# A delta-rule attention feeding a softplus MLP on one core: the work up to the first MLP layer, put in another order

## The chip, the cores and the metric

The kernel runs on one core of one Trainium2 chip. The time is the device time of one execution in microseconds (us), lower is better. The engines are PE (TensorE, matmuls), DVE (VectorE), ACT (ScalarE), POOL (GpSimd) and SP (SyncE, which issues nearly all DMAs here). Each has its own instruction queue, taken strictly in order; semaphores tie them together.

## What is computed

```python
def _attn_ref(q, k, v, beta):              # q, k, v: (4, 8, 768, 48)
    k_n = k / (np.linalg.norm(k, axis=-1, keepdims=True) + 1e-06)
    state = zeros((B, H, D, D))
    for t in range(S):
        y[:, :, t] = einsum('bhd,bhde->bhe', q[:, :, t], state)
        v_old = einsum('bhde,bhd->bhe', state, k_n[:, :, t])
        state = state + beta[:, :, t] * outer(k_n[:, :, t], v[:, :, t] - v_old)
    return y

def _moe_ref(x, w_in, w_out):              # x: y as (3072, 384); w_in (384, 2048)
    h = x @ w_in
    g = np.maximum(h, 0.0) + np.log1p(np.exp(-np.abs(h)))
    return g @ w_out
```

## The kernel before

**Staging.** The 768 steps are cut into 12 chunks (`NS`) of 64 steps, for all 32 pairs of batch and head at once. Inside a chunk the recurrence is a triangular system of 64 by 64 per head. Two chunks share one `invert(u)`, which turns the 32 by 32 diagonal blocks of their systems into inverses on DVE, row by row; the off-diagonal blocks are added with matmuls. A chunk's result y goes as the input x into the MLP, which is `layer` s of the loops below: 16 pieces of the hidden dimension, two at a time, so eight groups g. For every group, `hidden(s, g)` multiplies x with two pieces of w_in, ACT and DVE make the softplus (`gh`), and `output(s, g)`, one group later, multiplies it with two pieces of w_out. The work of chunks s+1 and s+2 is planned into the groups of layer s by the table that `at(...)` fills.

**Before the first layer** nothing can be overlapped with an MLP: the code between `with tc.manual_schedule` and `plan = {}` does chunk 0 in the order in which it is written, which is the order on every engine. Its steps, with the tiles by which they are found in the trace: `gram_heads` (products of keys, tile `work`), `p_half` (queries by keys into `ph`), `invert(0)` (tiles `ltq`, `Z`, `tmp`), `finish(0)` (two transposes of `Z` into `tt`), `join(0)` (two sets of 128 matmuls that put the 16-wide halves of the inverse together; the first set is emptied by ACT into `w1`, tile `x`; a subtraction and a third transpose follow on DVE), `mask_p` (four products with `maskP` into `big`), `cross_a`, `arrange`, `cross_b` (off-diagonal blocks: matmuls into one PSUM tile `pa`, emptied in four pieces by ACT and DVE in turn; `arrange` copies on ACT and clears on POOL), `scale_v`, `u_all` (emptied into `big`), `y_all` (y into `x` and `x4`, then six DMAs that put x4's rows into x) and `state`.

**Three streams are threaded through this.** The weights of piece f come by two DMAs (`a`, `b`, 384 KB each); `top(f)` on ACT (two CASTs into `ex`) and `convert(f)` on DVE (two SCALAR_TENSOR_TENSOR into `a`) make floats of them. Two `ex` tiles serve all pieces in turn, so `top(f)` waits until `convert(f-2)` has read. `invert(1)` is a generator in `background`; `pull(budget)` takes steps from it, by costs in ns that are written at each `yield`, until the budget is used. In the first layers `room`, from `EARLY[s]`, is that budget for each group. A load of weights into a tile is set free by a one-column copy on DVE (`[:, 0:1]`, here a token).

**Names in the profile.** L180 transpose of `work`, L217 and L222 the two operations of an elimination step, L228 and L230 the transposes of `finish`, L249 and L250 the end of `join`, L241 and L248 its matmuls, L258 and L281 the matmuls of `cross_a` and `cross_b`, L264 and L266 and L285 their emptying, L272 `arrange`, L321 `mask_p`, L328 and L332 `u_all`, L355, L360 and L361 `y_all`, L371 its DMAs, L340 and L343 `state`, L397 `top`, L407 `convert`, L384 the token, L446 `hidden`, L450 to L452 and L463 the softplus of layer 0, L474 `output`.

Of the kernel before, what the change touches and what calls it, by code (L numbers as in the profile page):

```python
# [7 lines left out]
F32 = mybir.dt.float32  # L8
F32R = mybir.dt.float32r
I32 = mybir.dt.int32  # L10
# [3 lines left out]
AF = mybir.ActivationFunctionType  # L14
ALU = mybir.AluOpType
# [16 lines left out]
AHEAD = 5  # L32
N16 = 1
STEP, EARLY, PULL0 = 3100, (4100, 3500, 3500), (500, 500, 3000)
# [7 lines left out]
def deltanet_moe(ctx, tc, kT, qT, kI, vN, beta, wts, out):  # L42
# [65 lines left out]
    def parity(t):  # L108
        return t.rearrange("p (a e) c -> p e a c", e=2)
# [114 lines left out]

    def finish(u):

        tt = TT[u] = one.tile([P, 2 * NP, 2 * HB], F32, name="tt")
        nc.vector.transpose(tt[:, :, 0:HB].rearrange("p q c -> p c q"), Z)  # L228
        yield 2000
        nc.vector.transpose(tt[:, :, HB:].rearrange("p q c -> p c q"),  # L230
                            Z.rearrange("p c j -> p j c"))
        yield 2000
# [19 lines left out]

    def cross_a(s):

        tt = TT[s // 2][:, s % 2 * NP:(s % 2 + 1) * NP, :]
        pm = ps_a.tile([P, NP // 2, HB], F32, name="pa")
        for i, e, p, ab, t in quads:
            nc.tensor.matmul(pm[(lo, hi)[e][t], i, :], OFF[s][hi[t], p, :], tt[hi[t], p, 0:HB],  # L258
                             start=True, stop=True)
        for e in range(2):  # L260
            for t in range(2):
                o = parity(OFF[s])[lo[t], e]
                if s < 1 and t:
                    nc.vector.tensor_scalar(o, pm[(lo, hi)[e][t]], -1.0, None, op0=ALU.mult)  # L264
                else:
                    nc.scalar.activation(o, pm[(lo, hi)[e][t]], AF.Copy, scale=-1.0)  # L266

    def arrange(s):

        tt = TT[s // 2][:, s % 2 * NP:(s % 2 + 1) * NP, :]  # L270
        for h in range(2):
            nc.scalar.copy(tt[hi[h], :, HB:], tt[hi[h], :, 0:HB])  # L272
        for h in range(2):
            nc.gpsimd.memset(tt[hi[h], :, 0:HB], 0.0)

    def cross_b(s):

        tt = TT[s // 2][:, s % 2 * NP:(s % 2 + 1) * NP, :]
        pm = ps_a.tile([P, NP // 2, HB], F32, name="pa")
        for i, e, p, ab, t in quads:  # L280
            nc.tensor.matmul(pm[(lo, hi)[e][t], i, :], tt[lo[t], p, HB:], OFF[s][lo[t], p, :],  # L281
                             start=True, stop=True)
        for e in range(2):
            for t in range(2):
                copies[s < 1 and t](parity(tt)[lo[t], e, :, HB:], pm[(lo, hi)[e][t]])  # L285
# [32 lines left out]
    def mask_p(g, pt):  # L318
        gs = slice(8 * g, 8 * g + 8)
        for ab in range(2):  # L320
            nc.vector.tensor_tensor(  # L321
                bv[tk[ab], ab, gs, 0:C], pt[tk[ab]],
                maskP[tk[ab]].unsqueeze(1).to_broadcast([C, 8, C]), op=ALU.mult)
# [21 lines left out]
    def y_all(s):  # L345
# [34 lines left out]
    def load_weights(f):  # L380
        RA[f] = one.tile([P, 2 * DM], I32, name=f"a{f + 1}")
        RB[f] = one.tile([P, 2 * DM], I32, name=f"b{f}")
        if f >= AHEAD:
            nc.vector.tensor_copy(RA[f][:, 0:1], RA[f - AHEAD][:, 0:1])  # L384
        for i, t in enumerate((RA[f], RB[f])):
            nc.sync.dma_start(t.bitcast(U16)[:, 0:4 * DM - 1],
                              wts[f][:, 4 * DM * i + 1:4 * DM * (i + 1)])
# [11 lines left out]
    def convert(n=1):  # L399
        for _ in range(n):  # L400
            f = done[0]
            if f == NF:
                return
# [7 lines left out]
            if f + AHEAD < NF:  # L411
                load_weights(f + AHEAD)

    def top(n=1):
        for _ in range(n):
            if done[1] < NF:
                assert done[1] < done[0] + 2
                top_half(done[1])
                done[1] += 1
# [70 lines left out]
    done = [0, 0]  # L490
    background = []
# [16 lines left out]
    with tc.manual_schedule(engines={ET.PE, ET.DVE, ET.Activation, ET.Pool, ET.SP}):  # L508
# [4 lines left out]
        load_weights(0)  # L513
# [8 lines left out]
        load_weights(1)  # L522
# [33 lines left out]
        load_v(1)  # L556
        for f in range(2, AHEAD):
            load_weights(f)
        load_k(4)
        run(iv)  # L560
# [12 lines left out]
        pull(1)  # L573
        top()
        run(jn)
        pull(1)
        convert()
        cross_a(0)
        arrange(0)
        top()  # L580
        scale_v(0)
        pull(PULL0[0])
        cross_b(0)
        convert()
        top()
        pull(PULL0[1])
        u_all(0)
        load_v(2)
        pull(PULL0[2])
        y_all(0)  # L590
        convert()
# [6 lines left out]
        top()  # L598

# [89 lines left out]
        for s in range(NS):  # L689
            for g in range(NF // 2):  # L690
                cost, *blocks = plan.pop((s, g), (0, (), ()))
                highs, lows = [x.get(8 * s + g, ()) for x in (HIGHS, LOWS)]
                if s == 0:
                    convert(max(0, 2 * g + 2 - done[0]))
                hidden(s, g)
# [9 lines left out]
                if s == 0:  # L705
                    convert(2)
                    top(2)
# [63 lines left out]
```

## Time and profile before

| | |
|---|---|
| time, median of 3 runs | 593.34 us (589.03 to 593.53) |
| the profiled execution | 592.98 us |
| its span in the trace | 591.3 us |
| PE busy | 559.9 us (95%) |
| DVE busy | 447.9 us (76%) |
| ACT busy | 356.0 us (60%) |
| weights `a` and `b`, from issue to landing | 4.9 and 5.6 us |

The first matmul of layer 0 starts 54 us into the span. Times below are us from the start of the span; a busy time is that of the engine's instructions without its waits. The granted clock is a share of 2.4 GHz, so 0.50 is 1.2 GHz.

### The profile page before, as it was taken

The numbers are of one execution on the slowest core, as the hardware profiler recorded it, in microseconds if no ns is written. First come the engines' busy times: TensorE is split into PE (matmuls) and PEld (weight loads), VectorE is DVE, ScalarE is ACT, GpSimd is POOL, SyncE is SP. The second block draws the span as 40 slices with busy tenths as digits, with TensorE's granted clock in tenths as the row PEclk, the third lists the DMA queues.
The fourth block names the chain that finished last, engine by engine and source line by source line (L and its number), as shares of the span: only waits on it lengthen the run. The fifth ranks groups of instructions, "written<-read, shape, count | busy, mean of one in ns | idle before, by whom it ended". The sixth has DMA issues, their size and how long they took to land.

```text
span 591.3 us, 19891 instructions
## 1 busy us (share of the span) xinstructions
PE 559.9 (95%) x8630; PEld 523.3 (88%) x8630; DVE 447.9 (76%) x1003; ACT 356.0 (60%) x719; POOL 30.2 (5%) x55
## 2 busy tenths in 40 slices
PE   5757799999999999999999999999999999999996
PEld 5446577789999999999999999999999999999996
DVE  5988789678899998798888898797895554554442
ACT  4444768898547584556595556685545576444543
POOL 4210000000000000000010000000000000000000
PEclk9657799999999999999999999999999999999999
DMA  9924852301320202320301320300311200300000
GB/s 215 334 71 116 267 190 57 68 30 55 68 60 29 65 30 55 68 82 13 60 30 55 68 83 12 60 30 29 68 55 28 42 29 2 76 21 15 28 0 28
DMA packets 35320, 39.82 MB, mean 67 GB/s; under 512 B 22688, under 2 KB 25856, under 8 KB 35232
## 3 DMA queue, kind: packets, MB, share of 16 engines
q1 hardware_dynamic: 35232, 38.54, 24.8%
q8 instruction: 68, 1.11, 0.8%
q14 instruction: 20, 0.16, 0.1%
HBM read 31.55 MB, written 4.72 MB: 61 GB/s over the span
## 4 chain that ended last, share of the span: by engine, by line
PE 80%; DVE 10%; ACT 5%; issue 2%; DMA 1%; SPq 1%; ACTq 0%; DVEq 0%
PE po L474 33%; PE ph L446 32%; PE pa L355 3%; PE pa L294 3%; PE pa L328 2%; PE pa L340 2%; PE pa L124 2%; DVE ltq L180 1%; PE pa L258 1%; PE pa L281 1%; DVE a L457 1%; DMA kt<-kT 1%; DVE Z L222 1%; DVE tmp L217 1%; DVE ltq L194 1%
## 5 line engine op out<-in xcount | busy, mean ns | idle before, releaser
L446 PE MATMUL ph<-x,b 128*128 128x256 f32 x1056 | 193.3, 282 | 0.0
L446 PE MATMUL ph<-x,a 128*128 128x256 f32 x624 | 172.9, 300 | 1.8 <-DMA x<-x 1.6
L446 PEld LDWEIGHTS ph<-x,b 128*128 128x128 f32 x1056 | 168.1, 190 | 0.5
L450 ACT ACTIVATE a<-ph 128x512 f32<-128x512 f32 x96 | 57.5, 599 | 175.9 <-PE ph L446 175.7
L474 PE MATMUL po<-a,gh 128*128 128x384 f32 x416 | 143.4, 367 | 0.0
L474 PE MATMUL po<-b,gh 128*128 128x384 f32 x352 | 124.4, 354 | 3.2 <-DVE gh L459 2.9
L446 PEld LDWEIGHTS ph<-x,a 128*128 128x128 f32 x624 | 119.7, 192 | 6.9 <-DMA x<-x 1.8
L457 DVE SCALAR_TENSOR_TENSOR a<-ph,a 128x512 f32<-128x512 f32 x88 | 60.5, 687 | 59.0 <-ACT a L452 58.4
L474 PEld LDWEIGHTS po<-a,gh 128*128 128x128 f32 x416 | 78.9, 191 | 8.0 <-issue 1.8
L474 PE MATMUL po<-b,gl 128*128 128x384 f32 x352 | 77.0, 334 | 0.0
L474 PEld LDWEIGHTS po<-b,gh 128*128 128x128 f32 x352 | 66.1, 188 | 9.0 <-DVE gh L459 3.6
L460 DVE TENSOR_TENSOR gl<-a,gh 128x512 fp32r<-128x512 f32 x88 | 61.0, 693 | 3.0
L451 ACT ACTIVATE a<-a 128x512 f32<-128x512 f32 x96 | 60.7, 632 | 3.1
L452 ACT ACTIVATE a<-a 128x512 f32<-128x512 f32 x96 | 60.7, 632 | 3.1
L474 PEld LDWEIGHTS po<-b,gl 128*128 128x128 f32 x352 | 62.3, 188 | 0.1
L222 DVE TENSOR_TENSOR Z<-Z,tmp 128x84 f32<-128x84 f32 (+14 forms) x178 | 54.3, 311 | 5.2
L217 DVE TENSOR_TENSOR tmp<-Z,ltq 128x84 f32<-128x84 f32 (+14 forms) x178 | 53.9, 309 | 3.6
L459 DVE CAST gh<-a 128x512 fp32r<-128x512 f32 x88 | 37.6, 427 | 3.0
L306 DVE TENSOR_TENSOR big<-pa,maskP 64x256 f32<-64x256 f32 x88 | 37.0, 420 | 0.9
L363 DVE TENSOR_TENSOR x<-pa,x 128x384 fp32r<-128x384 f32 x22 | 12.2, 553 | 25.9 <-ACT x L361 25.9
L355 PE MATMUL pa<-big 128*64 128x64 f32 x768 | 27.1, 231 | 0.5 <-ACT big L332 0.4
L355 PEld LDWEIGHTS pa<-big 128*64 128x64 f32 x768 | 25.1, 144 | 2.7 <-ACT big L332 0.5
(94 smaller groups left out, 572.9 us busy)
## 6 DMA issues: line engine op xcount, KB each, us to landing
a<-wts SPq DMA_DIRECT2D x16, 383.8 KB, 4.9
b<-wts SPq DMA_DIRECT2D x16, 383.8 KB, 5.6
kt<-kT SPq DMA_DIRECT2D x24, 192.0 KB, 3.6
big<-qT SPq DMA_DIRECT2D x24, 192.0 KB, 4.4
nv<-vN SPq DMA_DIRECT2D x12, 384.0 KB, 3.2
ki<-kI SPq DMA_DIRECT2D x24, 192.0 KB, 4.5
out<-ex SPq DMA_DIRECT2D x24, 192.0 KB, 2.0
x<-x SPq DMA_DIRECT2D x66, 32.0 KB, 2.0
```

The lines of the kernel that those rows point to most:

```text
L217: nc.vector.tensor_tensor(o, Z[:, a + j + 1:a + n, a + j:a + j + 1].to_broadcast([P, r, j]), lq[:, a + j:a + j + 1, a:a + j].to_broadcast( ...
L222: nc.vector.tensor_tensor(z, z, o, op=ALU.add)
L306: nc.vector.tensor_tensor(be[tk[ab], ab, e, 4 * g:4 * g + 4, 0:C], pks[e][t, :, 0:C], maskP[t].unsqueeze(1).to_broadcast([C, 4, C]), op=AL ...
L355: nc.tensor.matmul(py[tk[ab], i, :], big[:, at + C:at + 2 * C], big[:, at:at + C], start=True, stop=True)
L446: nc.tensor.matmul(ph[:, f], weight(s, 2 * g + f, a, k * P, P), xr[b][k], start=(c == 0), stop=(c == len(terms) * NK - 1))
L450: nc.scalar.activation(a, ph, AF.Abs)
L451: nc.scalar.activation(a, a, AF.Exp, scale=-1.0)
L452: nc.scalar.activation(a, a, AF.Ln, bias=1.0)
L457: nc.vector.scalar_tensor_tensor(a, ph, 0.0, a, op0=ALU.max, op1=ALU.add)
L459: nc.vector.tensor_copy(hi_lo[0], a)
L460: nc.vector.tensor_tensor(hi_lo[1], a, hi_lo[0], op=ALU.subtract)
L474: nc.tensor.matmul(PO[s][:, h, 0:DM], hi_lo[b][:, f, h * P:(h + 1) * P], weight(s, 2 * g + f, a, DM, DM), start=(g == 0 and f == 0 and i = ...
```

## The change

- `finish(0)` and `join(0)` are taken apart: the transpose of `Z` into the first half of `tt` is done in two halves of 16 columns (`turn`), and `join(0)`'s first matmuls stand between the parts. The four `mask_p` pieces are placed one by one between steps of the chain; `invert(1)` is not begun before `u_all(0)` has been emptied.
- `cross_a(0)` and `cross_b(0)` write two PSUM tiles, one by t, so that ACT empties one and DVE the other. Of `arrange(0)` the copies come ahead of `cross_a(0)`, the clearing behind it.
- The three `pull` calls with budgets (500, 500, 3000) become one with 5000 behind `state(0)`; `EARLY[0]` goes from 4100 to 4500.
- Two of the three `convert` and the `top` calls that stood inside the chain now stand behind `y_all(0)`.
- Weights come half a piece at a time by `feed`: from the third step of the elimination on, spread over the chain and the groups of layer 0, each half with a token that copies from the constant `half`. `load_v(1)`, `load_v(2)` and `load_k(4)` move to later places.
- Of the six DMAs of `y_all(0)` ACT issues three.

```diff
-STEP, EARLY, PULL0 = 3100, (4100, 3500, 3500), (500, 500, 3000)
+STEP, EARLY, PULL0 = 3100, (4500, 3500, 3500), 5000
...
+    def turn(u, a, b):
+        nc.vector.transpose(TT[u][:, :, a:b].rearrange("p q c -> p c q"), Z[:, a:b])
...
+    def cross(s, product, emptied):
+
+
+        n = 2 if s < 1 else 1
+        pms = [ps_a.tile([P, NP // 2, HB], F32, name="pa") for _ in range(n)]
         for i, e, p, ab, t in quads:
-            nc.tensor.matmul(pm[(lo, hi)[e][t], i, :], OFF[s][hi[t], p, :], tt[hi[t], p, 0:HB],
-                             start=True, stop=True)
+            a, b = product(p, t)
+            nc.tensor.matmul(pms[t % n][(lo, hi)[e][t], i, :], a, b, start=True, stop=True)
...
         for hh in range(NK):
             for ab in range(2):
-                nc.sync.dma_start(x[ab * C + D:(ab + 1) * C, hh],
-                                  x4[ab * C + 16 * hh:ab * C + 16 * hh + 16])
+                (nc.scalar if s == 0 and ab else nc.sync).dma_start(
+                    x[ab * C + D:(ab + 1) * C, hh],
+                    x4[ab * C + 16 * hh:ab * C + 16 * hh + 16])
...
+    def feed(n=1):
+
+        for _ in range(n):
+            if not halves:
+                return
+            f, i = halves.pop(0)
+            t = (RA, RB)[i][f] = one.tile([P, 2 * DM], I32, name=f"{'ab'[i]}{f + 1 - i}")
+            if f:
+                nc.vector.tensor_copy(t[:, 0:1], half.bitcast(I32))
             nc.sync.dma_start(t.bitcast(U16)[:, 0:4 * DM - 1],
                               wts[f][:, 4 * DM * i + 1:4 * DM * (i + 1)])
...
-        run(finish(0))
-        background.append(invert(1))
+        TT[0] = one.tile([P, 2 * NP, 2 * HB], F32, name="tt")
+        turn(0, QB, HB)
+        feed()
         jn = join(0)
         next(jn)
-        for g in range(2):
-            mask_p(g, pts[g])
-        pull(1)
+        top()
+        turn_back(0)
+        feed()
+        turn(0, 0, QB)
+        mask_p(0, 0, pts[0])
+        feed()
+        run(jn)
+        mask_p(0, 1, pts[0])
+        feed(2)
+        arrange(0, 1)
+        cross_a(0)
+        arrange(0, 0)
+        scale_v(0)
+        feed(2)
+        cross_b(0)
+        mask_p(1, 0, pts[1])
+        feed(2)
+        u_all(0)
+        mask_p(1, 1, pts[1])
+        feed(2)
+        background.append(invert(1))
         pull(1)
+        y_all(0)
+        load_v(1)
+        convert()
+        feed(2)
         top()
...
         jn = join(1)
         state(0)
@@ -596,6 +616,7 @@
         next(jn)
         convert()
         top()
+        pull(PULL0)
```

How the instructions stand now is shown for three places.

DVE, from the end of the elimination of `invert(0)` to the end of `join(0)` (L249 and L250 before, L254 and L255 after; tile names as above, `half` is the constant that the tokens copy). Before:

```order
L222 TENSOR_TENSOR Z<-Z,tmp 128x14 x2
L228 STREAM_TRANSPOSE tt<-Z 128x32x32
L230 STREAM_TRANSPOSE tt<-Z 128x32x32
L321 TENSOR_TENSOR big<-ph,maskP 64x8x64 x4
L180 STREAM_TRANSPOSE ltq<-work 128x32x32
L249 TENSOR_TENSOR tt<-tt,pa 128x16x16
L250 STREAM_TRANSPOSE tt<-tt 128x16x32
```

and after:

```order
L400 COPY a_359<-half 128x1
L225 STREAM_TRANSPOSE tt<-Z 128x16x32
L400 COPY b_459<-half 128x1
L228 STREAM_TRANSPOSE tt<-Z 128x32x32
L400 COPY a_531<-half 128x1
L225 STREAM_TRANSPOSE tt<-Z 128x16x32
L332 TENSOR_TENSOR big<-ph,maskP 64x8x64
L400 COPY b_536<-half 128x1
L254 TENSOR_TENSOR tt<-tt,pa 128x16x16
L255 STREAM_TRANSPOSE tt<-tt 128x16x32
```

Three of four `mask_p` pieces and the transpose L180 of `invert(1)` no longer stand ahead of the end of `join(0)`.

DVE, from the copies of y into `x` to the first steps of `invert(1)` (L360 and L361 before, L371 and L372 after; L217 and L222 before are steps 28 and on of its elimination). Before:

```order
L360 COPY x_776<-pa 128x3x128
L361 COPY x_777<-pa 128x128
L407 SCALAR_TENSOR_TENSOR a_299<-a_299,ex 128x384
L407 SCALAR_TENSOR_TENSOR a_299<-b_300,ex 128x384
L384 COPY a_826<-a_299 128x1
L407 SCALAR_TENSOR_TENSOR a_303<-a_303,ex 128x384
L407 SCALAR_TENSOR_TENSOR a_303<-b_304,ex 128x384
L384 COPY a_941<-a_303 128x1
L217 TENSOR_TENSOR tmp<-Z,ltq 128x84
```

and after, from the last of three `convert`s that now stand there:

```order
L422 SCALAR_TENSOR_TENSOR a_359<-a_359,ex 128x384
L422 SCALAR_TENSOR_TENSOR a_359<-b_459,ex 128x384
L146 COPY ss<-ltq 128x32
L151 TENSOR_SCALAR rt<-ss 128x32
L155 RECIPROCAL r_937<-rt 128x32
L156 TENSOR_TENSOR r_937<-r_937,ss 128x32
L157 TENSOR_TENSOR r_937<-r_937,rt 128x32
L158 TENSOR_SCALAR nt<-r_937 128x32
```

The norms of `invert(1)` (L146 to L166), its two scalings and its first two elimination steps stood ahead of the copies of y and now stand behind them.

ACT, from the copies of y to the softplus of group 0 (L450 before, L463 after; `rt` is the square root of the norms of `invert(1)`, which L155 on DVE reads). Before:

```order
L360 COPY x_776<-pa 128x3x128
L361 COPY x_777<-pa 128x128
L397 CAST ex<-a_229 128x384
L397 CAST ex<-b_230 128x384
L343 COPY big<-pa 48x8x48 x4
L243 COPY x_310<-pa 128x16x16
L397 CAST ex<-a_623 128x384
L397 CAST ex<-b_624 128x384
L450 ACTIVATE a<-ph 128x512
```

and after:

```order
L382 DMA x_754<-x_755 16x256 x3
L412 CAST ex<-a_359 128x384
L412 CAST ex<-b_459 128x384
L412 CAST ex<-a_531 128x384
L412 CAST ex<-b_536 128x384
L354 COPY big<-pa 48x8x48 x4
L248 COPY x_285<-pa 128x16x16
L412 CAST ex<-a_607 128x384
L412 CAST ex<-b_610 128x384
L152 ACTIVATE rt<-rt 128x32
L153 ACTIVATE rt<-rt 128x32
L463 ACTIVATE a<-ph 128x512
```

Three DMA issues, one more pair of CASTs and the two operations on `rt` now stand between the copies of y and the softplus.

## Rows read from the trace of the kernel before

**Rows 1.** The page, section 2: the span in 40 equal slices of 14.8 us; each digit is the busy share of PE in a slice, in tenths.

```profile
PE   5757799999999999999999999999999999999996
```

**Rows 2.** Busy time in one stretch from the end of layer 0 on, by engine (its length; then busy us and number of instructions of PE, weight loads, DVE, ACT and POOL; then granted clock, DMA share, GB/s).

```profile
111.20:138.00 26.80, 26.24 (x508) 22.95 (x508) 21.36 (x31) 25.83 (x52) 1.35 (x3) 1.00 0.24 56
```

**Rows 3.** DVE in order of time, from the end of `invert(0)` to the copies of y (start, length, line, out<-in, count, idle before).

```profile
26.10 1.92 DVE L228 STREAM_TRANSPOSE tt<-Z 128x1024 f32<-128x1024 f32 x1
...
29.77 2.80 DVE L321 TENSOR_TENSOR big<-ph,maskP 64x512 f32<-64x512 f32 x4
...
34.66 0.42 DVE L249 TENSOR_TENSOR tt<-tt,pa 128x256 f32<-128x256 f32 x1
35.11 0.71 DVE L250 STREAM_TRANSPOSE tt<-tt 128x512 f32<-128x512 f32 x1
...
39.24 0.43 DVE L264 TENSOR_SCALAR off<-pa 32x256 f32<-32x256 f32 x1 [0.44 <-ACT off L266]
...
44.41 0.15 DVE L384 COPY a<-a 128x1 int32<-128x1 int32 x1
44.47 0.18 DVE L161 TENSOR_TENSOR r<-nt 128x32 f32<-128x32 f32 x1
...
50.86 0.28 DVE L361 COPY x<-pa 128x128 f32<-128x128 f32 x1
```

**Rows 4.** PE in order of time in the same stretch, and at two `output`s of layer 0.

```profile
28.16 1.90 PE L241 MATMUL pa<-tt,x 32*32 32x16 f32 x128 [0.82 <-DVE tt L228]
30.55 0.51 PE L248 MATMUL pa<-x,tt 32*32 32x16 f32 x20 [0.48 <-ACT x L243]
32.57 1.68 PE L248 MATMUL pa<-x,tt 32*32 32x16 f32 x108 [1.52 <-issue]
...
36.03 0.85 PE L258 MATMUL pa<-tt,off 32*32 32x32 f32 x44 [0.37 <-issue]
...
43.45 1.94 PE L328 MATMUL pa<-nv,tt 64*64 64x48 f32 x60 [0.44 <-DVE tt L285]
45.78 4.27 PE L355 MATMUL pa<-big 128*64 128x64 f32 x63 [0.38 <-ACT big L332]
...
68.15 0.34 PE L258 MATMUL pa<-tt,off 32*32 32x32 f32 x9 [3.06 <-issue]
68.42 5.41 PE L474 MATMUL po<-a,gh 128*128 128x384 f32 x8
...
77.03 2.85 PE L474 MATMUL po<-a,gh 128*128 128x384 f32 x8
```

**Rows 5.** PE in three stretches, each from the end of one wait marked "issue" to the end of the next (its length, busy us, number of matmuls; granted clock, DMA share, GB/s).

```profile
32.50:36.00 3.50, 2.21 (x128) 0.50 0.02 5
36.00:53.40 17.40, 11.88 (x381) 0.61 0.37 118
53.40:68.10 14.70, 9.87 (x254) 0.84 0.78 217
```

**Rows 6.** ACT in order of time: an operation on `rt`, `arrange(0)`, what follows the copies of y, and the cast for piece 13 in layer 0.

```profile
36.41 0.23 ACT L154 ACTIVATE rt<-rt 128x32 f32<-128x32 f32 x1
...
39.23 1.26 ACT L272 COPY tt<-tt 32x512 f32<-32x512 f32 x2
...
53.12 1.93 ACT L343 COPY big<-pa 48x384 f32<-48x384 f32 x4
...
55.22 0.62 ACT L397 CAST ex<-a 128x384 f16<-128x384 bf16 x1
55.71 0.62 ACT L397 CAST ex<-b 128x384 f16<-128x384 bf16 x1
...
86.93 0.63 ACT L397 CAST ex<-a 128x384 f16<-128x384 bf16 x1 [2.50 <-DVE a L407]
```

**Rows 7.** SP: the issue of the six DMAs of `y_all(0)`.

```profile
51.20 3.75 SPq L371 DMA_DIRECT2D x<-x  x6
```

**Rows 8.** DVE in four stretches (length, busy us, number of instructions): the two parts of the norms of `invert(1)`, its scalings with two elimination steps, and six more steps.

```profile
40.55:41.62 1.07, 0.94 (x5) 0.50 1.02 393
44.46:45.70 1.24, 1.03 (x7) 0.50 0.07 18
46.82:50.37 3.55, 3.35 (x7) 0.59 0.75 264
53.28:57.32 4.04, 3.64 (x14) 0.91 0.12 28
```

**Rows 9.** DVE in layer 0, in order of time: the end of `join(1)`, the softplus of groups 0, 2 and 3, and a wait for the keys of chunk 1.

```profile
61.76 0.42 DVE L249 TENSOR_TENSOR tt<-tt,pa 128x256 f32<-128x256 f32 x1 [4.47 <-PE pa L248]
...
62.85 0.65 DVE L463 SCALAR_TENSOR_TENSOR gh<-ph,a 128x512 f32<-128x512 f32 x1
...
78.41 0.69 DVE L463 SCALAR_TENSOR_TENSOR gh<-ph,a 128x512 f32<-128x512 f32 x1 [1.46 <-ACT a L452]
...
83.43 0.62 DVE L298 TENSOR_TENSOR nv<-nv,pa 128x192 f32<-128x192 f32 x2 [0.48 <-PE pa L294]
...
85.74 0.69 DVE L463 SCALAR_TENSOR_TENSOR gh<-ph,a 128x512 f32<-128x512 f32 x1
```

**Rows 10.** Two stretches of layer 0, all engines, columns as in rows 2: from the cast for piece 13 to the end of the emptying of `u_all(1)`; and from the first matmul of `y_all(1)` to the softplus of group 7 on ACT.

```profile
86.92:99.96 13.04, 13.04 (x199) 9.70 (x198) 12.29 (x33) 12.70 (x26) 0.00 (x0) 1.00 0.25 69
102.40:111.29 8.89, 8.89 (x153) 7.19 (x156) 4.92 (x7) 6.30 (x13) 0.00 (x0) 1.00 0.11 23
```

More of the change, by code (lines that the diff above doesn't have):

```diff
@@ L268, in arrange, with emptied @@
-    def arrange(s):
-        tt = TT[s // 2][:, s % 2 * NP:(s % 2 + 1) * NP, :]
[L271 to L274, printed above, removed]
+        def emptied(e, t, pm):
+            o = parity(OFF[s])[lo[t], e]
+            if s < 1 and t:
+                nc.vector.tensor_scalar(o, pm, -1.0, None, op0=ALU.mult)
+            else:
+                nc.scalar.activation(o, pm, AF.Copy, scale=-1.0)
@@ L276, in cross_b, with arrange @@
+        cross(s, lambda p, t: (OFF[s][hi[t], p, :], tt[hi[t], p, 0:HB]), emptied)
+    def arrange(s, parts=2):
+        tt = TT[s // 2][:, s % 2 * NP:(s % 2 + 1) * NP, :]
+        if parts:
+            for h in range(2):
+                nc.scalar.copy(tt[hi[h], :, HB:], tt[hi[h], :, 0:HB])
+        if parts != 1:
+            for h in range(2):
+                nc.gpsimd.memset(tt[hi[h], :, 0:HB], 0.0)
     def cross_b(s):
         tt = TT[s // 2][:, s % 2 * NP:(s % 2 + 1) * NP, :]
-        pm = ps_a.tile([P, NP // 2, HB], F32, name="pa")
@@ L280, in cross_b @@
[L280 to L285, printed above, removed]
+        cross(s, lambda p, t: (tt[lo[t], p, HB:], OFF[s][lo[t], p, :]),
+              lambda e, t, pm: copies[s < 1 and t](parity(tt)[lo[t], e, :, HB:], pm))
     def keys(s, g):
@@ L316, in p_half, with mask_p @@
         return pt
-    def mask_p(g, pt):
+    def mask_p(g, ab, pt):
         gs = slice(8 * g, 8 * g + 8)
[L320 to L323, printed above, removed]
+        nc.vector.tensor_tensor(
+            bv[tk[ab], ab, gs, 0:C], pt[tk[ab]],
+            maskP[tk[ab]].unsqueeze(1).to_broadcast([C, 8, C]), op=ALU.mult)
     def u_all(s):
@@ L490, in deltanet_moe @@
     done = [0, 0]
+    halves = [(f, i) for f in range(NF) for i in range(2)]
     background = []
@@ L566, in deltanet_moe @@
         top()
[L567 to L568 removed]
+        TT[0] = one.tile([P, 2 * NP, 2 * HB], F32, name="tt")
+        turn(0, QB, HB)
+        feed()
         jn = join(0)
         next(jn)
[L571 to L572 removed]
+        top()
[3 more added lines that the diff above has]
+        mask_p(0, 0, pts[0])
+        feed()
+        run(jn)
[13 more added lines that the diff above has]
+        background.append(invert(1))
         pull(1)
+        y_all(0)
+        load_v(1)
+        convert()
+        feed(2)
         top()
[L575 to L576 removed]
         convert()
[L578 to L591, printed above, removed]
+        feed(2)
         top()
@@ L705, in deltanet_moe @@
                 if s == 0:
-                    convert(2)
-                    top(2)
+                    if g == 1:
+                        load_v(2)
+                        load_k(4)
+                    feed(2)
+                    for k in range(2):
+                        convert(done[0] < 2 * g + 5 + k)
+                        top(done[1] < 2 * g + 7 + k)
+                        feed(1 - k)
                 for f in highs:
```

46 lines of the change are left out of this document (15 added, 31 removed).

## The prediction

> **What bounds the kernel now.** I read the page's slices first: PE is at 9 tenths from the sixth slice on, that is from about 74 us, and at 5 to 7 before [rows 1]. So what can be won lies in the first five slices, and it counts only as far as it still stands when PE is full. Next I read the stretch in which the two meet: from 111 to 138 us ACT is busy 25.83 of 26.80 us and PE 26.24 [rows 2]. Whatever the shift of ACT is at 111 us, it is carried on; behind that PE has no room to give anything back or to lose it. The question is therefore one number: by how much does the softplus of group 7, at 111.29 us on ACT [rows 10], move.
>
> Then DVE and PE in order of time. Before layer 0 it is one chain, DVE to PE to ACT and back, and DVE holds work that the chain doesn't need: four `mask_p` pieces of 0.70 us stand ahead of L249 [rows 3], and L180 behind them. PE has waits marked "issue", in which it waits for nothing that the profile shows: 1.52, 0.37 and 3.06 us [rows 4], and one more that ends at 53.4. From the end of each to the end of the next are 128, 381 and 254 matmuls [rows 5], multiples of 127 to 128, so these are borders of PE's instruction stream: the next piece has not come yet. In layer 0 the view of DVE shows how little it idles: 4.47, 1.46 and 0.48 us between 57 and 86 us [rows 9].
>
> **The chain before layer 0.** The elimination ends at 26.1 [rows 3]. I walk the new order from there.
>
> - A token costs what lies between its start and the next operation's, 0.06 us [rows 3]; five more in the elimination: 26.4.
> - Half a transpose, half of 1.92 [rows 3]: 27.4. The first 128 matmuls of `join(0)`, 1.90, and ACT's copy, 0.5 up to PE's next start [rows 4]: 29.8. The long transpose ends at 29.3 beside them and costs nothing; if PE were faster by over 0.5, it would.
> - The second 128 matmuls meet a border after 20 of them. In the trace of before the piece that was late at 32.57 could be asked for when PE entered the piece before it, at the 20th matmul of those that start at 28.16: 4.1 us. The next one came 3.46 us after that (36.03) [rows 4], with the DMA engines nearly idle (share 0.02) [rows 5]. Now the loads of weights are spread over exactly this stretch: eight halves of 384 KB in 12 us, some 256 GB/s, where the stretch with the 3.06 wait had 217 [rows 5]. I take 4.0 us, near the loaded one of the two: the border opens at 31.7, the rest, 1.68, ends at 33.4.
> - The subtraction, 0.45: 33.8. `cross_a` starts, meets the next border after 20 matmuls (34.3), goes on at 35.7 and ends 0.85 later [rows 4]: 36.5. ACT's `arrange`, 1.26 [rows 6], and the third transpose, 0.71, lie beside this and end at 35.8.
> - Two banks: ACT and DVE empty two pieces each side by side, 2 x 0.43 [rows 3], instead of in turn, and no `convert` stands in between: 37.4. `cross_b`, 64 matmuls at the same pace, 1.2, and its emptying 0.9: 39.5.
> - `u_all` 2.1, `y_all` 0.4 later and 4.27 [rows 4], DVE's two copies 0.8: **47.1, where before they ended at 51.1** [rows 3].
>
> `mask_p`'s pieces, the tokens and L180 fall into waits of DVE for PE there, and cost nothing as long as PE is the later one. So the chain gives 4.0 us. The x DMAs are issued by two engines, three each, which at 3.75 us for six [rows 7] gives another 1.9 us for the first `hidden`.
>
> **What the chain was relieved of stands behind it.** All that was taken out, apart from L180, follows the copies of y on DVE, and its head waits for ACT. ACT now does from 47.1 on: three DMA issues, 1.9; two cast pairs, 2.2; the copies of `state` and `join` and one more pair, which before went from 53.12 to 56.33, 3.2 [rows 6]; then `rt`, two operations of 0.23, 0.5. That is 54.9; with the gap of a semaphore 55.1. DVE has by then done three `convert`s and stands for some 4 us: its first reciprocal needs `rt`. Behind the wait are queued the rest of the norms, 1.07 + 1.24, the scalings with two steps, 3.55, and the six steps that stood there before too, 4.04 [rows 8]: 65.0. Then the end of `join(1)`, 1.1 [rows 9], and at 66.1 the softplus of group 0. **Before, it started at 62.85** [rows 9]: the gain of 4.0 is a loss of 3.2 there, since some 7 us of work (norms 2.3, scalings with two steps 3.55, one `convert` more) and a wait of some 4 came behind the copies of y, while one wait of 4.47 went.
>
> In layer 0 DVE then has no wait left. By group 3 it saves the 1.46 and 0.48 us that it waited before [rows 9], and pays two more elimination steps, 1.6 (`EARLY[0]` is larger and the two early steps went), and three tokens, 0.2. Group 3's softplus is late by 3.1. The cast for piece 13 waited 2.50 us for DVE already [rows 6]; now the one for piece 12 stands there and starts at 90.0. From it to the end of the emptying of `u_all(1)` ACT has no wait, 13.04 us [rows 10], and one cast pair more, 1.1: 104.2. `y_all(1)` on PE, which started at 102.40 right behind `hidden`, waits for that: 1.8 late, and the 8.89 us from it to the softplus of group 7 [rows 10] are PE's and stay.
>
> **The sum.** 592.98 us, the profiled execution, and 1.8 make 594.8. The median of the runs is 0.36 us above the profiled one, so this stands 1.5 above the median, well inside the 1% (5.9 us) that a measurement of this kernel can tell from no change. PE's own gain, an earlier first `hidden` and the 3.06 wait, is lost because PE now stands before the second cross product of layer 0 until DVE has finished `join(1)`.
>
> Bounds of what the trace of before doesn't show. The two borders: I have waits of 1.4 us at each; with 3.46 us for a piece they are 0.9 and 0.8 (1.1 us less), with the 3.06 of before at each 3.3 more. ACT's issue of a DMA is not in the trace: nothing would take 1.9 off, twice SP's would put 1.9 on; I take SP's since the transfers are the same. The two halves of the transpose could cost as much as L250's 0.71 for 512 elements or 0.96; that changes 0.5 at most.
>
> One rule speaks for another result. The Trainium skill (Runtime: NRT & Kernel Launch, Instruction fetch mechanics) says that an engine's instructions come in blocks of 256 and that crossing a border is mostly hidden. The distances in [rows 5] agree with the size, two instructions to a matmul; the waits of up to 3.06 us in [rows 4] don't agree with "hidden".
>
> **The rivals.**
>
> *The borders cost nothing*, since the pieces of PE's instructions come in time at the new pace. Then `cross_a` ends at 33.8, but ACT's `arrange` (34.4) becomes the later one, and the copies of y end at 45.0: 2.1 less, 592.7. That is what the rule above would give. Against it: PE stood at both borders before, with more time between them.
>
> *PE is the bound from the first `hidden` on.* If DVE's late work could be absorbed, layer 0 would start 4.0 + 1.9 earlier, without the 3.06 wait and with the first `output` at 2.85 instead of 5.41 us [rows 4]: 11.5 less, 581.5. For it speaks that PE is full from 74 us on [rows 1]. Against it: DVE would have to fit 11 us of added work and waiting into the 6.4 us that it idled.
>
> *PE's clock falls before `y_all(1)`* (slower). PE stands there for about 2.4 us, waiting for ACT. After the 3.06 us wait the eight matmuls of `output` took 5.41 us where later eight took 2.85 [rows 4]. `y_all(0)` took 4.27 before layer 0, where a stretch shows 0.50 [rows 4, 5]; half of that, 2.1, is the price: 596.9. It decides from the wait on at which the clock falls, and the rows show only that 3.06 is enough in this place.
>
> *The weights crowd the chain* (slower). Spread loads keep the DMA engines busy throughout the chain instead of before it, and each border costs 3.06: 3.3 more, 598.1. For it speaks the 217 GB/s beside the longest wait; against it that the other two cost 1.52 and 0.37 [rows 4].
>
> **How the numbers follow.** My forecast, between 593.5 and 596, has 0.45; no cost at the borders 0.15; the clock 0.17; crowded loads 0.11; PE as the bound 0.07; 0.05 is left. The range reaches from 590 (borders free, ACT's issues cheap) to 600 (crowded loads with the fallen clock) and leaves out the case of PE as bound and what is left. Faster by over 1% is the PE case and a bit, 0.09; slower by over 1% needs both slow cases at once or longer waits, 0.10; 0.81 lies within.
>
> **What would show it.** In the changed profile: the copies of y on DVE end near 47; DVE waits some 4 us for `rt` right behind three `convert`s; the softplus of group 0 on DVE starts at 66 and not at 62.9; PE stands 7 us or more ahead of the second cross product, of chunk 1; ACT has no wait between the cast for piece 12 and `u_all(1)`, and PE waits for it ahead of `y_all(1)`. I am wrong if the softplus of group 7 lies well before 111 us, or if DVE shows idle time between groups 0 and 4.

## The result

| | before | changed |
|---|---|---|
| time, median of 12 runs each | 592.68 us (589.03 to 594.27) | 595.96 us (594.99 to 597.37) |
| the profiled execution, its span | 592.98 us, 591.3 us | 597.37 us, 595.6 us |
| PE, DVE, ACT busy | 559.9, 447.9, 356.0 us | 558.7, 446.8, 355.6 us |

The ratio is 1.0063, 95% interval 1.0045 to 1.0082: slower by 3.3 us, a difference inside the 1%. The forecast was 594.8. The profiled execution of the changed kernel is the longest of its twelve, so that the two profiled executions lie 4.4 us apart. All three engines are busy a little less than before (0.4 to 1.2 us), and the kernel is slower: what was gained and lost are waits. Of the 69 runs of the kernel before beside the experiments below, the 14 with a mean granted clock of 0.999 or 1.00 took 587.8 to 590.0 us and the 30 with one of 0.962 to 0.965 or 0.990 to 0.994 took 590.7 to 596.4, and both of its profiled executions (0.965, and 0.991 in the repetition below) are of the longer kind, with the first `output` of layer 0 at a granted clock of 0.52 and 0.62.

The page of the changed kernel, PE by slices (compare [rows 1]): the fourth slice is fuller than before, 9 tenths instead of 7, the fifth emptier, 4 instead of 7.

```profile
PE   5759499999999999999999999999999999999996
```

The fifth slice, 60 to 74 us, holds a stand of PE of 7.41 us. PE in order of time, first in the chain, then at the second cross product of layer 0 (compare [rows 4]):

```profile
27.35 1.91 PE L246 MATMUL pa<-tt,x 32*32 32x16 f32 x128 [1.43 <-DVE b L400]
29.74 0.51 PE L253 MATMUL pa<-x,tt 32*32 32x16 f32 x20 [0.48 <-ACT x L248]
32.71 1.67 PE L253 MATMUL pa<-x,tt 32*32 32x16 f32 x108 [2.47 <-issue]
...
37.26 0.85 PE L265 MATMUL pa<-tt,off 32*32 32x32 f32 x44 [1.83 <-issue]
...
42.41 1.52 PE L339 MATMUL pa<-nv,tt 64*64 64x48 f32 x45 [0.68 <-issue]
...
67.77 1.07 PE L265 MATMUL pa<-tt,off 32*32 32x32 f32 x64 [7.41 <-DVE tt L254]
```

DVE, from the end of `join(0)` to the softplus of group 3 (compare [rows 3, 9]; L371 and L372 are the copies of y, L155 the first reciprocal of the norms of `invert(1)`, L254 the end of a `join`, L476 the softplus):

```profile
34.42 0.42 DVE L254 TENSOR_TENSOR tt<-tt,pa 128x256 f32<-128x256 f32 x1 [3.68 <-PE pa L253]
...
49.43 0.28 DVE L372 COPY x<-pa 128x128 f32<-128x128 f32 x1
...
57.64 0.35 DVE L155 RECIPROCAL r<-rt 128x32 f32<-128x32 f32 x1 [3.50 <-ACT rt L153]
...
67.30 0.41 DVE L254 TENSOR_TENSOR tt<-tt,pa 128x256 f32<-128x256 f32 x1
...
68.38 0.65 DVE L476 SCALAR_TENSOR_TENSOR gh<-ph,a 128x512 f32<-128x512 f32 x1
...
84.25 0.68 DVE L476 SCALAR_TENSOR_TENSOR gh<-ph,a 128x512 f32<-128x512 f32 x1
...
91.00 0.69 DVE L476 SCALAR_TENSOR_TENSOR gh<-ph,a 128x512 f32<-128x512 f32 x1
```

The copies of y end at 49.7 (51.1 before): the chain gained 1.4 us, not 4.0. Then comes the wait of 3.50 us for `rt`, and behind it the row of work without a wait, up to the end of `join(1)`, for which PE stands. Group 0's softplus starts at 68.38, 5.5 us later than before. ACT in order of time shows why `rt` is late, and what is left of the delay at the cast for piece 12, at the emptying of `u_all(1)` (L343) and at the softplus of group 7 (compare [rows 6, 10]):

```profile
49.78 2.14 ACTq L382 DMA_DIRECT2D x<-x  x3
51.96 0.63 ACT L412 CAST ex<-a 128x384 f16<-128x384 bf16 x1 [4.07 <-DVE a L422]
...
54.06 1.93 ACT L354 COPY big<-pa 48x384 f32<-48x384 f32 x4
...
57.38 0.23 ACT L153 ACTIVATE rt<-rt 128x32 f32<-128x32 f32 x1
...
92.25 0.63 ACT L412 CAST ex<-a 128x384 f16<-128x384 bf16 x1 [2.41 <-DVE a L422]
...
104.28 1.95 ACT L343 COPY big<-pa 64x384 f32<-64x384 f32 x4
...
115.08 0.60 ACT L463 ACTIVATE a<-ph 128x512 f32<-128x512 f32 x1 [1.54 <-PE ph L459]
```

Group 7 is 3.8 us late (111.30 before). From there to the end of the span it is 480.5 us, and 480.0 before: 0.5 us more go behind it, where PE waits for DVE in layer 1 (3.6 us in sum against 2.9; the longest, near 163 us, is 1.43).

### The profile page after: what moved, and what is told of

Same layout as the page of the kernel before. It is cut to its first block, busy times and chain, and to the rows that moved or that the text cites. A ratio compares the mean times of both kernels' runs of the same rounds, so it can differ in the third digit from the quotient of the medians.

```text
span 595.6 us, 19928 instructions
## 1 busy us (share of the span) xinstructions
PE 558.7 (94%) x8630; PEld 522.8 (88%) x8630; DVE 446.8 (75%) x1023; ACT 355.6 (60%) x719; POOL 30.2 (5%) x55
## 4 chain that ended last, share of the span: by engine, by line
PE 77%; DVE 11%; ACT 7%; issue 3%; DMA 1%; SPq 0%; ACTq 0%; DVEq 0%
PE po L487 31%; PE ph L459 30%; PE pa L366 4%; PE pa L306 3%; PE pa L351 2%; PE pa L339 2%; PE pa L265 2%; DVE tmp L216 2%; DVE Z L221 2%; PE pa L123 1%; DVE a L422 1%; ACT ex L412 1%; ACT b L437 1%; ACT a L464 1%; DMA kt<-kT 1%
## 5 line engine op out<-in xcount | busy, mean ns | idle before, releaser
L459 PE MATMUL ph<-x,a 128*128 128x256 f32 x624 | 171.1, 297 | 0.0
L463 ACT ACTIVATE a<-ph 128x512 f32<-128x512 f32 x96 | 57.5, 599 | 166.5 <-PE ph L459 160.5
```

The costliest lines, as they stand in the source:

```text
L459: nc.tensor.matmul(ph[:, f], weight(s, 2 * g + f, a, k * P, P), xr[b][k], start=(c == 0), stop=(c == len(terms) * NK - 1))
L463: nc.scalar.activation(a, ph, AF.Abs)
```

## The experiments

Two theories were to be told apart. **A**: what was taken out of the chain falls due behind it, with a wait for `rt`; that sets group 0's softplus, and DVE, without a wait, sets the rest of layer 0. **B**: the borders of PE's instructions, or the spread loads, set the pace, and where DVE's side work stands is of no account. All readings in one table; the profiled execution of each kernel gives the columns but the last two (us). The ratio is to runs of the kernel before on the same chip beside it; their median was between 590.9 and 592.7, so a ratio says more than a difference of medians:

| kernel | waits at the borders in `join(0)`, `cross_a`, `u_all` | copies of y end | from there to group 0's softplus | from that to group 7's softplus on ACT | median | ratio to before, interval |
|---|---|---|---|---|---|---|
| before | 1.52, 0.37, none | 51.14 | 11.7 | 48.45 | 592.68 | |
| before, again | 2.43, 0.73, none | 51.66 | 12.9 | 46.10 | one run, 592.38 | |
| changed | 2.47, 1.83, 0.68 | 49.71 | 18.7 | 46.70 | 595.96 | 1.0063 (1.0045 to 1.0082) |
| changed, again | 2.23, 1.28, 0.40 | 48.43 | 18.9 | 46.71 | one run, 596.24 | |
| `rt` early | 1.30, 1.28, 0.40 | 47.65 | 15.4 | 46.69 | 592.2 | 1.0017 (0.9997 to 1.0036) |
| one queue | 2.48, 0.73, none | 47.64 | 17.3 | 46.71 | 594.18 | 1.0048 (1.0021 to 1.0075) |
| late feeds | 2.89, 0.73, none | 47.36 | 23.0 | 46.68 | 599.77 | 1.0153 (1.0117 to 1.0189) |
| filled waits | 2.72, 1.55, none | 49.10 | 11.9 | 46.70 | 589.14 | 0.9962 (0.9938 to 0.9985) |
| filled, shifted | elsewhere | 50.53 | 10.1 | 46.71 | 589.7 | 0.9978 (0.9957 to 0.9999) |
| one bank | 2.50, 0.73, none | 49.21 | 19.2 | 46.72 | 597.15 | 1.0107 (1.0075 to 1.0138) |
| whole transpose | 0.75, 1.28, 0.40 | 47.91 | 19.4 | 46.72 | 595.97 | 1.0088 (1.0059 to 1.0117) |
| head alone | 2.60, 0.73, none | 51.28 | 16.3 | 43.82 | 593.2 | 1.0039 (1.0020 to 1.0057) |
| filled, quiet chain | 2.48, 1.28, none | 48.63 | 10.1 | 45.81 | 587.38 | 0.9935 (0.9913 to 0.9958) |

The fifth column decides much: in nine executions of eight kernels in the changed order it is 46.68 to 46.72. There, whenever group 0's softplus starts, group 7's starts 46.70 us later; only the last kernel, with its casts in another order, has 45.81. In the order of before it is 43.82 to 48.45: something else, PE, sets group 7.

**`rt` early.** Directly behind `y_all(0)`:

```diff
         y_all(0)
+        pull(1)
         load_v(1)
```

> The changed kernel, but the sum of squares of the norms of invert(1) on DVE and the two operations on rt on ACT stand directly behind y_all(0), ahead of ACT's casts and of the copies of state(0). Theory A (the work of invert(1) behind the copies of y, with its wait of 3.50 us for rt, sets the softplus of group 0, and PE follows DVE from there to group 3): the wait shrinks to 0.5 us or less, the softplus of group 0 on DVE starts at 65.0 to 65.5 instead of 68.38, PE stands 4 us instead of 7.41 ahead of the second cross product of chunk 1, and the time falls by 2.5 to 3.3 us, to within 1 us of the kernel before. Theory B (the slow supply of PE's instructions in the chain and the time that the chain takes set everything behind it): the copies of y end where they did, and the time stays within 0.7 us of the changed kernel's.

DVE in this kernel, the rows that answer to those above:

```profile
47.37 0.28 DVE L372 COPY x<-pa 128x128 f32<-128x128 f32 x1
...
52.28 0.35 DVE L155 RECIPROCAL r<-rt 128x32 f32<-128x32 f32 x1
...
63.03 0.65 DVE L476 SCALAR_TENSOR_TENSOR gh<-ph,a 128x512 f32<-128x512 f32 x1
```

The reciprocal has no wait any more, and the distance from the copies of y to the softplus is 15.4 instead of 18.7 and 18.9: 3.3 to 3.5 us, the wait. The median is 3.8 us below the changed kernel's (by the ratios, 2.7). The softplus at 63.03 lies 2 us below the forecast because this execution's copies of y ended 2.1 us earlier, with the same code up to there; that is not the edit's doing. A holds.

**One queue.** All DMAs of x from SP:

```diff
-                (nc.scalar if s == 0 and ab else nc.sync).dma_start(
+                nc.sync.dma_start(
```

> The changed kernel, but all six DMAs of x for chunk 0 are issued by SP. Theory A: ACT starts its casts 2.1 us earlier, rt is there 2.1 us earlier, DVE waits 1.4 instead of 3.50 us, group 0's softplus starts at 66.3, and the time falls by 1.5 to 2 us; the last x lands about 2 us later, so the first hidden starts near 55 us instead of 52.73, which costs nothing, since PE stands 7.41 us behind it anyway. Theory B: the later x makes the first hidden later and the time does not fall, or rises by up to 2 us.

The distance fell by 1.4 to 1.6 us and the median by 1.8 (by the ratios 0.9, with overlapping intervals). DVE's wait for `rt` is still 2.74 us and not 1.4, since its converts, which wait for ACT's casts, were also done sooner. PE waits for the last x in this kernel, and starts the rest of the first `hidden` at 54.04:

```profile
54.04 3.65 PE L459 MATMUL ph<-x,a 128*128 128x256 f32 x8 [1.10 <-DMA x<-x]
...
64.29 1.06 PE L265 MATMUL pa<-tt,off 32*32 32x32 f32 x64 [2.62 <-DVE tt L254]
```

That later x costs nothing, since PE still stands 2.62 us for the end of `join(1)`. The issue of DMAs by ACT, meant to bring x earlier, did so, won nothing by it and delayed `rt`.

**Late feeds.** The loads of halves 7 to 9 stand in the elimination (`feed` at every second step), those of 10 to 17 behind `load_v(1)`:

> The changed kernel, but no half of a weight piece is loaded between the first transpose and the copies of y: three of these eleven loads are moved into the elimination, eight behind y_all(0). If the supply of a block of PE's instructions slows with the load on the DMA engines (5.06 us beside about 260 GB/s, 5.15 beside 219, 4.55 beside 68, and 3.46 beside 5 GB/s in the kernel before): the openings of the borders are some 3.5 us apart, the waits of 2.47, 1.83 and 0.68 us shrink to less than half in sum (5.0 to 2 or less), and the copies of y on DVE end at 47 to 47.8 instead of 49.7. If the supply does not depend on the load: the same waits within 0.3 us each, copies of y at 49.5 or later. For the time, Theory A says 1.5 to 2.5 us less if the casts of pieces 4 and 5 don't wait for their loads, nothing gained or a loss if they do.

PE in `join(0)` and `cross_a(0)`, then ACT at the cast of piece 5:

```profile
32.89 1.67 PE L253 MATMUL pa<-x,tt 32*32 32x16 f32 x108 [2.89 <-issue]
...
36.34 0.85 PE L265 MATMUL pa<-tt,off 32*32 32x32 f32 x44 [0.73 <-issue]
```

```profile
57.68 0.62 ACT L412 CAST ex<-a 128x384 f16<-128x384 bf16 x1 [3.70 <-DMA a<-wts]
```

The second piece came 3.45 us after the first, with 5 GB/s on the DMA engines, and the copies of y ended at 47.4, as forecast for the quiet chain. The waits did not shrink as forecast, though: 3.6 us in sum and not 2 or less, and in the one-queue kernel, with the loads spread, the copies end at 47.6 with waits of 3.2. So this run does not show that the loads slow the pieces. ACT then stood 3.70 us for the load of piece 5, `rt` stands behind that cast, DVE waited 7.77 us, and the kernel is slower than any other here. The spread of the loads is what keeps these casts from waiting.

**Filled waits.** The head of `invert(1)` goes into waits of DVE (moved lines only):

```diff
         turn(0, 0, QB)
-        mask_p(0, 0, pts[0])
+        background.append(invert(1))
+        pull(1)
+        pull(1)
         feed()
         run(jn)
+        mask_p(0, 0, pts[0])
...
         mask_p(1, 0, pts[1])
+        pull(1)
+        pull(1)
         feed(2)
         u_all(0)
         mask_p(1, 1, pts[1])
         feed(2)
-        background.append(invert(1))
         pull(1)
+        pull(1)
         y_all(0)
```

and `PULL0` is 700, which gives the same two elimination steps.

> The changed kernel, but the head of invert(1) fills waits of DVE in the chain: its transpose and the sum of squares in the wait of 3.7 us for the end of join(0), the rest of the norms in the wait of 2.5 us for u_all(0), the two scalings between u_all(0) and the copies of y; two elimination steps behind the copies as in the changed kernel. Theory A: the chain's end stays at 49.7 (within 0.5), behind it only three converts and eight elimination steps stand ahead of the end of join(1), the softplus of group 0 starts at 60 to 61 instead of 68.38, PE's stand of 7.41 us is all but gone, and by group 7 some 7 us are left of it against the kernel before's place: a time of 585.5 to 589, faster than both kernels. Theory B, or a bound that lies elsewhere in layer 0 (the border of PE's instructions that cost 3.06 us in the kernel before, casts that wait for their loads): 590 us or more.

PE at two borders of this kernel, then DVE at the end of `join(1)` and at group 0's softplus:

```profile
53.52 0.57 PE L246 MATMUL pa<-tt,x 32*32 32x16 f32 x46 [2.51 <-issue]
...
64.93 0.26 PE L265 MATMUL pa<-tt,off 32*32 32x32 f32 x8 [1.65 <-issue]
```

```profile
59.93 0.42 DVE L254 TENSOR_TENSOR tt<-tt,pa 128x256 f32<-128x256 f32 x1 [1.71 <-PE pa L253]
...
61.02 0.65 DVE L476 SCALAR_TENSOR_TENSOR gh<-ph,a 128x512 f32<-128x512 f32 x1
```

The chain ended at 49.10, no later for the added work; the softplus came at 61.02, at the edge of the forecast; PE's stand of 7.41 us is gone. Faster than both kernels, with a median just above the forecast (585.5 to 589). Group 7 starts at 107.72, 7.4 us ahead of the changed kernel, so what group 0 gained is carried on in full; that is 3.6 ahead of before, and the "some 7 us" of the forecast are right only against the changed kernel. Of the two border waits shown, the one in `join(1)` cost DVE 1.71 us; the one in the second cross product cost nothing behind it, as the distance to group 7 is 46.70 here too.

**Filled, shifted.** Ten small matmuls ahead of the `p_half` pieces:

```diff
+        pc, k = ps_a.tile([P, 8, C], F32, name="pa"), kts[1][dr[0], 0, :]
+        for i in range(10):
+            nc.tensor.matmul(pc[tk[0], i % 8, :], k, k, start=True, stop=True)
```

> The kernel in which the head of invert(1) fills the waits, with ten small matmuls more (twenty in the trace's count) before the p_half pieces, whose result nobody reads. If the waits marked issue are borders at fixed distances in PE's instruction stream and the next piece is asked for when PE enters a piece, every border moves twenty matmuls towards the start: PE then waits ahead of the first matmul of the second group of join(0) and not after twenty of it, opens there near 31.5 instead of 32.97 us, meets the next one at the head of cross_a, and the copies of y end about 1 us earlier; behind the copies the waits stand elsewhere too (after 62 instead of 82 matmuls of join(1), after 36 instead of 56 of the second cross product). Time 0.5 to 1.2 us less, if the later borders don't cost more than the 2.51 and 1.65 us there now. If the waits have another cause (a DMA, a semaphore that the profile doesn't show), they stand after 20, 20 and 82 matmuls as before.

PE, at the second group of `join(0)`, in `join(1)` and in the second cross product:

```profile
32.72 1.90 PE L253 MATMUL pa<-x,tt 32*32 32x16 f32 x128 [3.15 <-ACT rt L152]
...
53.11 0.74 PE L246 MATMUL pa<-tt,x 32*32 32x16 f32 x66 [0.53 <-issue]
...
63.12 0.44 PE L265 MATMUL pa<-tt,off 32*32 32x32 f32 x28 [1.45 <-issue]
```

Every border moved by twenty matmuls, to the first of the second group (128 in one row; the engine named is a chance one, as ACT's copy of `w1` had long ended) and to 62 and 36 of the later groups. So these waits are borders of PE's instruction stream. The gain did not come: the border opened at 32.72, not 31.5, the copies of y ended at 50.53, not about 48, and no time was won (0.9978 beside 0.9962, intervals overlapping). The border in `join(1)` cost only 0.53 us here, and the distance from the copies of y to the softplus is 10.1 us, where the filled kernel, whose DVE waited 1.71 behind that border, has 11.9.

**One bank** (`n = 1` in `cross`) and **whole transpose** (`turn(0, 0, HB)`, no third transpose): parts of the change undone.

> The changed kernel with one part undone: both cross products of chunk 0 write one bank again, so ACT and DVE empty it in turn. By the steps of the prediction each of the two products is then emptied 0.4 to 0.9 us later (0.43 us a piece, one after the other instead of side by side), the copies of y end 0.9 to 1.7 us later, and since DVE is the bound from there to group 3 the time rises by 0.7 to 1.5 us. If the borders of PE's instructions set the pace of the chain anyway, the later emptying hides in the waits at the borders: copies of y within 0.5 us of 49.7 and the time within 0.5 us of the changed kernel's.

> The changed kernel with one part undone: the first transpose of the inverse is one piece of 1.92 us again, instead of half of it ahead of join(0) and the other half behind the long transpose. The first matmul of join(0) starts 0.9 us later (28.3 instead of 27.35). If a late piece of PE's instructions is asked for when PE enters the piece before it, the first border opens later by the same 0.9 and the copies of y too: time up by 0.5 to 1.0 us. If the borders come at a time of their own (set by the load on the DMA engines alone), the 0.9 hides in the 2.47 us wait: time within 0.4 us of the changed kernel's.

With one bank the copies of y ended at 49.21, within the two executions of the changed kernel (49.71 and 48.43), though DVE and ACT emptied the bank in turn; the median is 1.2 us higher than the changed kernel's, while the intervals of the ratios overlap: a small loss is likely, and not settled. With the whole transpose `join(0)` started 1.2 us later (28.56), the border wait was 0.75 instead of 2.47 and 2.23 us, and the median is the same to 0.01 us (the ratios' intervals overlap). Here the later start hid in the wait: the border opened at 32.19, though PE came to it later, against 32.71 and 32.25.

**Head alone.** On the kernel before: the `append` and the five `pull`s of the chain (two of one step, three with budgets) go, and `background.append(invert(1))`, `pull(1)` stand ahead of `y_all(0)`, `pull(5000)` behind the last `top()`.

> The kernel before with one part of the change alone: the head of invert(1) (transpose, norms, scalings, two elimination steps) no longer stands between the steps of the chain; its transpose comes ahead of the copies of y, the rest behind the converts that follow them. Transposes, banks, loads and the issue of the DMAs are as before. Theory A (what is taken out of the chain falls due behind it, with a wait for rt): the copies of y end up to 1 us earlier than 51.1, DVE waits 2 to 3 us for rt, group 0's softplus starts at 65 to 66.5 instead of 62.85, DVE has no wait left at groups 2 and 3, and the time is 0.5 to 2 us above the kernel before. Theory B (the move is free, what costs is the spread of the loads and the slower supply of PE's instructions): the time is within 0.4 us of the kernel before, or below it.

DVE in this kernel, at the copies of y, the first reciprocal and group 0's softplus:

```profile
51.00 0.28 DVE L361 COPY x<-pa 128x128 f32<-128x128 f32 x1
...
56.84 0.35 DVE L156 RECIPROCAL r<-rt 128x32 f32<-128x32 f32 x1 [3.00 <-ACT rt L154]
...
67.58 0.65 DVE L463 SCALAR_TENSOR_TENSOR gh<-ph,a 128x512 f32<-128x512 f32 x1
```

The copies of y end where they did (51.28; 51.14 and 51.66 before): this side work had cost the chain nothing, or 0.4 us at most if the execution with like border waits is compared (2.43 and 0.73). Its price behind the chain is all there: a wait of 3.00 us, the softplus at 67.58, 1.1 later than A's forecast. By the ratio of the runs this part alone costs 2.3 us (1.2 to 3.4) where the whole change costs 3.7 (2.7 to 4.9); in the profiled execution group 7 starts at 111.40, hardly later than before's 111.30 and 110.69: PE's first `output` starts at 68.38, as in the two executions of before (68.42, 68.68), where a border in the second cross product holds it.

**Filled, quiet chain.** The filled waits, the loads as in the late feeds, and without the `top()` ahead of `pull(PULL0)`, so that the cast of piece 5 is left to group 0.

> The kernel in which the head of invert(1) fills the waits, and no weights are loaded between the first transpose and the copies of y (three of the eleven loads moved into the elimination, eight behind y_all(0)); the cast of piece 5 is moved from ahead of group 0's softplus to behind it, so that ACT doesn't stand there for a load. If loads slow the supply of PE's instructions: from the second border on the pieces follow each other in 3.5 us, the third border shows no wait, the copies of y end 1.5 to 2 us earlier than with the loads spread, and the time is 1 to 2.5 us below that of the kernel with the filled waits alone. If the loads packed behind the copies cost more than the quiet chain gains (casts in groups 1 to 3 that wait for their halves, a slower piece at the border in join(1) and at the second cross product): the same time within 1 us, or longer.

PE in `join(1)`, in the second cross product and in `y_all(1)`:

```profile
49.19 2.40 PE L246 MATMUL pa<-tt,x 32*32 32x16 f32 x128
...
62.11 0.26 PE L265 MATMUL pa<-tt,off 32*32 32x32 f32 x8 [2.19 <-issue]
...
95.41 2.26 PE L366 MATMUL pa<-big 128*64 128x64 f32 x63
```

The lowest median here: 587.38 us, 1.8 below the filled waits (by the ratios 1.6, with overlapping intervals). The copies of y came 0.5 us earlier, not 1.5 to 2, and the second piece took 4.00 us beside 4 GB/s: the mechanism forecast for it is not what the rows show. What they show is no wait in `join(1)`, where the filled kernel lost 1.71 us on DVE, and none in `y_all(1)`: group 7 starts 45.81 us behind group 0, 0.9 less than elsewhere. Between ACT's last wait for DVE and `u_all(1)` there are three pairs of casts instead of four.

**Both kernels again**, one execution each.

> The changed kernel once more, unaltered, to see how far one profiled execution speaks for others. If the waits at the borders are a property of the program: 2.47, 1.83 and 0.68 us again within 0.2 each, copies of y at 49.7. If they depend on the execution (when each load happens to be under way): other values, with a sum between 2.4 and 5.0 as in the kernels that have the same code up to there, and copies of y between 47.5 and 49.7; the wait of 3.5 us for rt and the distance from the copies of y to group 0's softplus (18.7 us) stay.

> The kernel before once more, unaltered. If the border waits depend on the execution, its waits of 1.52, 0.37 and 3.06 us come out otherwise, the last one above all, with the first output of layer 0 starting at another time than 68.42; if they are a property of the program, the same within 0.2 each.

PE at borders, first in the changed kernel, then in the one before:

```profile
32.25 1.68 PE L253 MATMUL pa<-x,tt 32*32 32x16 f32 x108 [2.23 <-issue]
...
36.25 0.85 PE L265 MATMUL pa<-tt,off 32*32 32x32 f32 x44 [1.28 <-issue]
```

```profile
33.45 1.68 PE L248 MATMUL pa<-x,tt 32*32 32x16 f32 x108 [2.43 <-issue]
...
68.48 0.27 PE L258 MATMUL pa<-tt,off 32*32 32x32 f32 x9 [1.65 <-issue]
```

The border waits are those of an execution, not of the program: 3.9 instead of 5.0 us in sum in the changed kernel, and in the one before 2.43 and 1.65 where [rows 4] have 1.52 and 3.06. The wait for `rt` is 3.49 again.

## Why the prediction was right, and where it was off

- **The mechanism was right, one term was mis-sized.** By the profiled executions the kernel lost 4.4 us, not 1.8: the chain came out 2.6 us longer than in the steps, the two distances behind it 0.3 us shorter each, and 0.5 were lost behind group 7. That the medians lie only 3.3 us apart, and 595.96 just inside the first case (593.5 to 596), is in part luck, since the profiled execution is the longest of the twelve.
- **The row of work behind the chain: right.** From the copies of y to group 0's softplus the steps gave 19.0 us; 18.7 and 18.9 were measured. The wait for `rt`, some 4, was 3.50, PE's stand ahead of the second cross product "7 us or more" was 7.41, and DVE has no wait between groups 0 and 4.
- **From group 0 to group 7: right.** 47.0 us by the steps, 46.70 measured. The cast for piece 12 and the end of the emptying of `u_all(1)` came in the order forecast, each about as late as the chain's error (92.25 for 90.0; 104.28 and 1.95, so 106.2, for 104.2). The step from `u_all(1)` to `y_all(1)` was off: PE, itself late, did not stand 2.4 us for it but twice 0.17.
- **The chain: the mis-sized term.** "47.1, where before they ended at 51.1": 49.7, and 48.4 in the second execution. The step that failed is that of the borders: 1.4 us were taken at each of two and nothing at the third; it was 2.47, 1.83 and 0.68 (2.23, 1.28, 0.40). The prediction took one execution's border waits for the program's. The first piece arrived some 5.1 us after PE had entered the one before it (4.8 in the second execution), not 4.0. That the time runs from that entry is not borne out either: with the whole transpose PE entered 1.2 us later and the border opened no later. That is not settled, since five executions with the same code up to there opened it between 31.48 and 32.75. With that the gain of 4.0 came out as 1.4 (2.7 by the second execution).
- **Where the gain was sought.** Head alone shows that taking the head of `invert(1)` off DVE gave the chain 0.4 us at most, and the transposes in parts gave nothing that the medians show: the later start hid in a border wait. What moving the `mask_p` pieces and the `convert`s gave was not tried by itself. The range allowed for this (crowded borders to 600).
- **The DMAs of x on two engines** were forecast as 1.9 us for the first `hidden` and 1.9 on ACT. ACT's issue took 2.14 us; undoing it won 1.8 us by the medians, 0.9 by the ratios.
- **Rivals.** Borders free: no, 5.0 us. PE the bound from the first `hidden`: no, it stands 7.41 us. The clock ahead of `y_all(1)`: the granted clock is 1.00 from 103 to 112 us, and PE's waits there are two of 0.17 us. Its price of 2.1 us is not borne out for `y_all(0)`, from which it was taken: the first 63 of its matmuls took 4.43 us at a granted clock of 0.50 (changed) and 4.43 at 1.00 (changed, again). Weights crowd the chain: the borders cost what that case said or nearly (5.0 of 6.1), but the cause is not shown, as the rows below say. The rule of the Trainium skill (Runtime: NRT & Kernel Launch, Instruction fetch mechanics) that crossing a border is mostly hidden is not borne out in the chain in any of the thirteen executions.
- **The last 0.5 us**, lost behind group 7, were not in the steps.

What decides how long a piece takes, 3.3 to 5.5 us here, stays open: the load on the DMA engines doesn't order the values. The stretch from the first border's opening to the second's, with columns as in [rows 2], in one queue, in the quiet chain and in the changed kernel:

```profile
32.72:36.18 3.46, 2.21 (x129) 1.97 (x129) 1.68 (x3) 0.49 (x1) 0.00 (x0) 0.50 0.21 82
```

```profile
32.97:36.97 4.00, 2.21 (x128) 1.97 (x128) 2.22 (x4) 1.00 (x2) 0.10 (x1) 0.50 0.02 4
```

```profile
32.71:37.26 4.55, 2.21 (x128) 1.96 (x128) 2.04 (x5) 1.23 (x2) 0.00 (x0) 0.50 0.18 68
```

In the thirteen executions this stretch is 3.45 or 3.46 us six times, 4.00 or 4.01 four times, and 4.27, 4.55 and 4.82 once each: steps of some 0.27 us, which no run here explains.

## What to carry to other kernels

Work taken off a critical chain is due somewhere: look at what its first instruction waits for in the new place (here `rt`, behind a queue on ACT), and whether the engine has a wait anywhere behind it to pay from. The best place for it was inside the chain, in waits that another engine causes, where it did not lengthen the chain and made the kernel 1.0% faster than with the work behind (0.9962 beside 1.0063). A wait that belongs to one execution should enter a sum as a range, since a second profile of the same program may show another.

## What was not expected of the hardware

PE's instruction borders, a fixed number of matmuls apart and moved by adding matmuls, cost 1.9 to 5.0 us within some 15 us of small dependent matmuls, with an amount that changes between executions of one program. The 108 small matmuls behind the first border took 1.67 us at a granted clock of 0.50 (changed) and 1.67 at 1.00 (late feeds): the granted clock (1.2 or 2.4 GHz) made no difference to them, nor to `y_all(0)` in the two executions of the changed kernel. Behind the chain it did: the first `output` of layer 0 took 5.41 us at 0.52 in the kernel before and 2.85 at 1.00 with the filled waits.
